# Two layers behind block-recurrent attention: units in the order of chunks, first products between the attention's steps, sums from parts, another planner

## The chip, the cores and the metric

One core of a Trainium2 chip. Five engines work side by side, each through its own queue in order: TensorE (PE; its weight loads are listed as PEld), VectorE (DVE), ScalarE (ACT), GpSimd (POOL) and SyncE (SP), which issues most loads. The metric is the time of one execution on the device in microseconds. The kernel before takes 581.78 us, the median of 3 runs (581.52 to 581.89).

## The reference

Blockwise linear attention with decay (2 batches, 8 heads, 768 positions, head size 64, blocks of 64), then two feed-forward layers (1536 tokens, 512 to 2048 to 512), all float32.

```python
for b in range(nb):                                   # 12 blocks of 64
    intra = einsum('bhic,bhjc->bhij', qb, kb) * Dmask
    intra = einsum('bhij,bhjd->bhid', intra, vb)
    inter = einsum('bhid,bhde->bhie', qb * lam_pow, kv_state)
    out[:, :, sl] = intra + inter
    kv_state = lam_block * kv_state + einsum('bhsd,bhse->bhde', kb * rev_pow, vb)
x = out.transpose(0, 2, 1, 3).reshape(1536, 512)
h = x @ w1i; x = where(h > 0, h, exp(min(h, 0)) - 1) @ w1o
h = x @ w2i; x = (max(h, 0) + alpha * min(h, 0)) @ w2o
```

## The kernel before

**The products.** A float32 operand is split into a high part, rounded to the fast format fp32r, and a low part, the rest (`split`, L385). A product is then three matmuls: high by high, high by low, low by high. The 1536 tokens are three chunks of 512, each of four tiles of 128 (`CHUNK`, L33: the tile numbers in the order in which they stand in the chunk; tiles 0 to 5 are batch 0, tiles 6 to 11 batch 1). The 2048 hidden columns are eight pairs j of two blocks of 128. An *up* step (`plain`, L794) is six matmuls of 128x128 by 128x512, half of one block of h; `finish` (L757) applies the layer's function and writes g, split into parts. A *down* step (`down`, L878) is six matmuls that add to acc. For j of 1 and more the up products of chunks 1 and 2 together are one two by two block product done with seven products instead of eight (`seven`, L836, table `PRODUCTS`); it needs the sums T1 to T4 of the blocks B11, B21 (chunk 1) and B12, B22 (chunk 2), which `combine` (L456) makes from the unsplit values in acc, working in place, split again into parts. T4 stands where B12 stood, so its split is made later (`late`).

**The attention.** Six units of 128 positions, each for both batches (`units`, m = 0 to 5; a unit is one tile of each batch). A unit has the steps scores (s, L557, masked on VectorE into sm), state (t, L604, the sum over the unit's keys and values, added to the decayed state st), outputs (o, L644) and earlier (i, L668, the part from the blocks before), each 64 matmuls of 64x64. `earlier` then evicts a bank of PSUM: a cast to the high part on ScalarE, the low part on VectorE, and for m below 4 a copy of the unsplit value to acc. Units 0 to 3 fill chunks 1 and 2, units 4 and 5 chunk 0. `attend` (L951) yields the steps in the order t0 o0 s1 i0 t1 o1 s2 i1 and so on; the last steps are merged one by one with the up steps of chunks 1 and 2 for pair 0. Then come `combine`, the down weights of pair 0, the rest of pair 0 and 1 for chunk 0, and `seven(0, 1)` among the down steps that are left.

**Order and queues.** `build` (L964) writes down all steps. `Plan` runs through them with a price for each: TensorE keeps the order as written, the other engines take what is needed first, in the order that the plan's clock gives. Loads of the first part are chained on SP's queue (`behind`): q, k and v of units 0 and 1, w1i of pair 0, units 2 to 5, w1o of pair 0. Tiles share memory by tags: a unit's tiles lie where g, x0, wa1, wd0, qT1 and qT2 come later, and the temporary ut where the powers of lam and the state st[3] are.

Of the kernel before, what the change touches and what calls it, by code (L numbers as in the profile page):

```python
# [32 lines left out]
CHUNK = [[4, 10, 5, 11], [0, 1, 2, 3], [6, 7, 8, 9]]  # L33
# [10 lines left out]
class Op:  # L44
    def __init__(self, costs, run, late, shared, dma):
        self.costs, self.run, self.late, self.shared, self.dma = costs, run, late, shared, dma
        self.least = min(costs.values())
        self.after, self.before = set(), []
        self.heir, self.waits = None, 0
        self.left = 0  # L50
        self.need = 0.0
        self.begun = False


class Plan:

    LAT = 0.12
    SPARE = 8.0  # L60
    EASE = 0.3
    HOLD = 8.0
# [6 lines left out]
    def add(self, costs, run, reads=(), writes=(), late=0.0, shared=False, dma=False):  # L69
        op = Op(costs, run, late, shared, dma)  # L70
# [12 lines left out]
    def behind(self, a, b):  # L83

        a.heir, b.waits = b, 1

    def needs(self):

        pe = [op for op in self.ops if "PE" in op.costs]
        behind = dict(zip(pe, pe[1:]))  # L90
        left = {}
        for op in self.ops:
            for a in op.after:
                a.before.append(op)
        for op in self.ops:
            left[op] = len(op.before) + (op in behind) + (op.heir is not None)
        todo = [op for op in self.ops if not left[op]]
        ahead = dict(zip(pe[1:], pe))
        first = {op.heir: op for op in self.ops if op.heir}
        n = 0  # L100
        while todo:
            op = todo.pop()
            n += 1
            ends = [s.need - (0.0 if "PE" in op.costs and "PE" in s.costs else self.LAT)
                    for s in op.before]
            if op in behind:
                ends.append(behind[op].need)
            op.need = min(ends, default=0.0) - op.least - op.late
            if op.heir:
                op.need = min(op.need, op.heir.need - op.least)  # L110
            for a in [*op.after, *([ahead[op]] if op in ahead else []),
                      *([first[op]] if op.waits else [])]:
                left[a] -= 1
                if not left[a]:
                    todo.append(a)
        assert n == len(self.ops)
        return pe

    def run(self):
        pe = self.needs()  # L120
        for op in self.ops:
            op.left = len(op.after) + op.waits
# [3 lines left out]
        events, n = [], 0  # L126
        at, done, now, dma, shift = 0, 0, 0.0, 0.0, -pe[0].need

        def offer(op):
            nonlocal n  # L130
            for e in op.costs:
                if e != "PE":
                    heapq.heappush(ready[e], (op.need, n, op))
# [7 lines left out]
        def begin(e, op):  # L141
            nonlocal dma
            op.begun = True
            op.run(e)
            if op.heir:
                op.heir.left -= 1
                if not op.heir.left:
                    offer(op.heir)
            cost = op.costs[e]
            free[e] = now + cost  # L150
# [3 lines left out]
            if op.dma:  # L154
                dma = max(dma, now + 1.6) + op.late
                wake(dma + self.LAT, op)
            else:
                wake(now + cost + (0.0 if e == "PE" else self.LAT), op)

        for op in self.ops:  # L160
            if not op.left:
                offer(op)
        while done < len(self.ops):
            for e in self.ENGINES:
                if free[e] > now + 1e-9:
                    continue
                if e == "PE":
                    if at < len(pe) and not pe[at].left:
                        shift = now - pe[at].need
# [4 lines left out]
                while ready[e]:  # L174
                    item = heapq.heappop(ready[e])
                    op = item[2]
                    if op.begun:
# [4 lines left out]
                    if e == "POOL" and any(  # L182
                            x.shared and not x.begun and x is not op and x.need < op.need
                            and x.need + shift < now + op.costs[e] + self.HOLD for _, _, x in ready["DVE"]):
# [3 lines left out]
                    slack = op.need + shift - now  # L188
# [922 lines left out]
```

## Time and profile before

| | |
|---|---|
| median of 3 runs | 581.78 us |
| the profiled execution | 581.23 us |
| its span, first to last instruction | 579.3 us |
| TensorE busy | 550.4 us, 95% |
| VectorE, ScalarE, GpSimd busy | 383.0, 293.1, 339.2 us |
| granted TensorE clock, mean | 0.982 |

The profile is one execution. Busy time is shown by engine; idle time stands beside what ended it, "issue" where the profile shows no wait. The span leaves out about 2 us around the first and last instruction.

### The profile page before, as it was taken

To read this page: it belongs to the slowest core of one execution; us is meant where nothing else is said; L and a number is where in the kernel's file an instruction comes from. 1 tells how busy PE (TensorE), PEld (TensorE's weight loads), DVE (VectorE), ACT (ScalarE), POOL (GpSimd) and SP (SyncE) were. 2 spreads that over 40 slices of the span, in tenths; PEclk is the share of its full clock that TensorE was granted. 3 is DMA by queue.
4 is the path that set the end of the run, shared out by engine and by line. 5 is a ranking of instruction groups with operands and counts; after the bars stand their busy time and mean duration, and the time that the engine had idled before them with its cause. 6 is when DMAs were issued, how large, how long until landed. Compare 5 with 4: busy or idle time off the path is not lost.

```text
span 579.3 us, 9092 instructions
## 1 busy us (share of the span) xinstructions
PE 550.4 (95%) x3712; PEld 457.1 (79%) x3712; DVE 383.0 (66%) x494; ACT 293.1 (51%) x474; POOL 339.2 (59%) x231
## 2 busy tenths in 40 slices
PE   7557999899999999999999999999999999999997
PEld 6457787788888888888878878788888888888886
DVE  3346679955866675757884688467776776765464
ACT  2326668585746464646562554664453443534320
POOL 4457152658767566564475886767859293946020
PEclk9778999999999999999999999999999999999999
DMA  8992032103122212221240100222332222000013
GB/s 320 393 291 77 20 129 74 46 30 143 41 106 74 72 74 72 74 72 74 72 147 1 35 39 1 73 74 73 98 120 74 72 74 72 1 0 1 36 38 145
DMA packets 20012, 49.62 MB, mean 86 GB/s; under 512 B 1282, under 2 KB 1538, under 8 KB 19970
## 3 DMA queue, kind: packets, MB, share of 16 engines
q1 hardware_dynamic: 19696, 48.51, 24.3%
q8 instruction: 29, 0.48, 0.3%
q10 hardware_dynamic: 274, 0.52, 0.3%
q14 instruction: 13, 0.11, 0.1%
HBM read 45.88 MB, written 3.15 MB: 85 GB/s over the span
## 4 chain that ended last, share of the span: by engine, by line
PE 85%; DVE 9%; issue 4%; DMA 1%; ACT 1%; SPq 0%; ACTq 0%
PE ps L895 41%; PE ps L845 20%; PE ps L815 18%; PE ps L668 2%; PE ps L604 1%; PE ps L557 1%; PE ps L644 1%; DMA blk<-in_vk 1%; DVE g L382 1%; DVE wt L413 1%; DVE qbl L382 1%; DVE wt L416 1%; DVE wdl L382 1%; DVE ps L859 1%; DVE acc L906 1%
## 5 line engine op out<-in xcount | busy, mean ns | idle before, releaser
L906 DVE TENSOR_TENSOR acc<-ps,acc 128x512 f32<-128x512 f32 (+1 forms) x169 | 116.1, 687 | 93.5 <-PE ps L895 92.6
L382 POOL TENSOR_TENSOR g<-rt,g 128x512 fp32r<-128x512 f32 x81 | 121.2, 1503 | 90.1 <-ACT g L374 88.0
L895 PE MATMUL ps<-wdh,g 128*128 128x512 f32 (+1 forms) x388 | 118.7, 387 | 1.4 <-DVE g L382 1.4
L895 PE MATMUL ps<-g,wdh 128*128 128x512 f32 x384 | 118.3, 389 | 0.0
L762 ACT ACTIVATE rt<-ps 128x512 f32<-128x512 f32 x96 | 57.3, 599 | 107.8 <-DVE ps L859 62.6
L895 PEld LDWEIGHTS ps<-wdh,g 128*128 128x128 f32 x388 | 72.7, 188 | 16.7 <-DVE g L382 1.9
L895 PEld LDWEIGHTS ps<-g,wdh 128*128 128x128 f32 x384 | 72.1, 188 | 15.0
L895 PE MATMUL ps<-wdl,g 128*128 128x512 f32 (+1 forms) x194 | 75.1, 387 | 0.0
L895 PE MATMUL ps<-g,wdl 128*128 128x512 f32 x192 | 74.8, 390 | 0.2 <-DVE wdl L382 0.2
L374 ACT CAST g<-rt 128x512 fp32r<-128x512 f32 x96 | 59.3, 618 | 28.7 <-DVE rt L775 14.4
L382 POOL TENSOR_TENSOR wsl<-wt,wsh 128x1024 fp32r<-128x1024 f32 x13 | 32.3, 2484 | 48.1 <-ACT wsh L374 30.5
L779 DVE SCALAR_TENSOR_TENSOR rt<-rt,beta,ps 128x512 f32<-128x512 f32 x48 | 35.7, 744 | 30.2 <-ACT rt L762 30.1
L382 POOL TENSOR_TENSOR wt<-wt 128x256 f32<-128x256 f32 x54 | 41.1, 778 | 10.4 <-DVE wt L416 4.8
L416 DVE SCALAR_TENSOR_TENSOR wt<-raw,wt 128x1024 uint32<-128x1024 uint32 x32 | 46.3, 1450 | 0.0
L413 DVE SCALAR_TENSOR_TENSOR wt<-raw,wt 128x1024 uint32<-128x1024 uint32 x32 | 45.6, 1429 | 0.2
L374 ACT COPY ut<-ps 128x512 f32<-128x512 f32 x42 | 24.6, 587 | 36.3 <-PE ps L845 36.1
L382 POOL TENSOR_TENSOR wdl<-wt,wdh 128x1024 fp32r<-128x1024 f32 x13 | 37.2, 2861 | 8.9 <-ACT wdh L374 8.7
L895 PEld LDWEIGHTS ps<-g,wdl 128*128 128x128 f32 x192 | 36.0, 188 | 7.9 <-DVE wdl L382 0.6
L895 PEld LDWEIGHTS ps<-wdl,g 128*128 128x128 f32 x194 | 36.4, 188 | 7.4
L859 DVE TENSOR_TENSOR ps<-ps,ut 128x512 f32<-128x512 f32 x42 | 29.2, 697 | 14.5 <-PE ps L845 14.3
L815 PE MATMUL ps<-x0l,wah 128*128 128x512 f32 x128 | 38.8, 389 | 0.0
L775 DVE SCALAR_TENSOR_TENSOR rt<-rt,ps 128x512 f32<-128x512 f32 x48 | 32.5, 681 | 8.7 <-ACT rt L773 8.0
(116 smaller groups left out, 948.6 us busy)
## 6 DMA issues: line engine op xcount, KB each, us to landing
raw<-in_w1i SPq DMA_DIRECT2D x8, 1024.0 KB, 5.5
raw<-in_w1o SPq DMA_DIRECT2D x8, 1024.0 KB, 4.9
raw<-in_w2i SPq DMA_DIRECT2D x8, 1024.0 KB, 5.5
raw<-in_w2o SPq DMA_DIRECT2D x8, 1024.0 KB, 4.9
blk<-in_kqT SPq DMA_DIRECT2D x11, 512.0 KB, 10.8
blk<-in_vk SPq DMA_DIRECT2D x10, 512.0 KB, 10.9
out<-acc SPq DMA_DIRECT2D x11, 256.0 KB, 2.0
blk<-in_kqT ACTq DMA_DIRECT2D x1, 512.0 KB, 5.3
```

Source lines behind the costliest of these rows:

```text
L374: nc.scalar.copy(dst(), src())
L382: lambda e: on(e).tensor_tensor(out=dst(), in0=a(), in1=b(), op=alu),
L413: op({"DVE": vec(1024)}, lambda e: nc.vector.scalar_tensor_tensor(out=tu, in0=lower, scalar=29, in1=tu, op0=ALU.logical_shift_right, op1=A ...
L416: op({"DVE": vec(1024)}, lambda e: nc.vector.scalar_tensor_tensor(out=tu, in0=upper, scalar=0x80000000, in1=tu, op0=ALU.bitwise_and, op1=A ...
L762: op({"ACT": act(512, True)}, lambda e: nc.scalar.activation(rt(i), h(), AF.Relu, scale=-1.0), [b_h], [b_r])
L775: op({"DVE": vec(512)}, lambda e: nc.vector.scalar_tensor_tensor(out=rt(i), in0=rt(i), scalar=-1.0, in1=h(), op0=ALU.add, op1=ALU.max), [b ...
L779: op({"DVE": vec(512) + 0.06}, lambda e: nc.vector.scalar_tensor_tensor(out=rt(i), in0=rt(i), scalar=beta[:, f:f + 1], in1=h(), op0=ALU.mu ...
L815: nc.tensor.matmul(out=banks[k], lhsT=wa(s, w)[:, cc, q * 128:(q + 1) * 128], rhs=(both[t][x] if t else x0(x))[:, cc, :], start=i == 0, st ...
L845: nc.tensor.matmul(out=banks[k], lhsT=left(s, a, w)[:, cc, :], rhs=quad(b, x)[:, cc, :], start=bool(opens and i == 0), stop=bool(closes an ...
L859: op({"DVE": vec(512)}, lambda e: nc.vector.tensor_tensor(out=banks[to], in0=banks[k], in1=ut(u), op=ALU.add), [b_ps[k], b_ut[u]], [b_ps[to]])
L895: nc.tensor.matmul(out=p_, lhsT=lhs, rhs=rhs, start=i == 0, stop=i == 5)
L906: op({"DVE": vec(w)}, lambda _, a=a, p_=p_: nc.vector.tensor_tensor(out=a(), in0=p_, in1=a(), op=ALU.add), [b_ps[k], *b_a], b_a)
```

## The change

The units go to the chunks in the order in which they are made: units 0 and 1 are chunk 1, units 2 and 3 chunk 2, units 4 and 5 chunk 0 as before. A written list, STEPS, sets the attention's steps with up steps (p) and down steps (d) of pair 0 for chunks 1 and 2 among them. w1o of pair 0 is loaded and converted ahead of unit 3. `earlier` no longer copies to acc; `combine_parts` adds high and low parts back together in the tiles of ut and makes T1 to T4 from those. Outputs always use banks 4 and 5. Units 2, 3 and 5 lie in other tiles. The planner gives TensorE an order of its own (FREE), counts instructions to be fetched (steps), goes forward and back through the plan six times and keeps the best by its own clock; SPARE and HOLD are smaller.

```diff
-CHUNK = [[4, 10, 5, 11], [0, 1, 2, 3], [6, 7, 8, 9]]
+CHUNK = [[4, 10, 5, 11], [0, 6, 1, 7], [2, 8, 3, 9]]
...
-    SPARE = 8.0
+    SPARE = 5.0
     EASE = 0.3
-    HOLD = 8.0
+    HOLD = 2.0
+    ROUNDS = 6
+    FETCH = 80.0
+    AHEAD = 512.0
+    FREE = True
     ENGINES = ("PE", "SP", "ACT", "DVE", "POOL")
...
+    def simulate(self, first, back=False, log=None):
+        pe = self.pe[::-1] if back else self.pe
+        before = (lambda op: op.after) if back else (lambda op: op.before)
...
+            if op.steps:
+                stock = min(self.AHEAD, stock + self.FETCH * (now - seen))
+                cost = max(cost, (op.steps - stock) / self.FETCH)
+                stock, seen = stock + self.FETCH * cost - op.steps, now + cost
...
+                if e == "PE" and self.FREE:
+                    while ready[e]:
+                        op = heapq.heappop(ready[e])[2]
+                        if op not in begun:
+                            shift = now - first[op]
+                            begin(e, op)
+                            break
+                    continue
                 if e == "PE":
...
+    def run(self):
+        self.pe = [op for op in self.ops if "PE" in op.costs]
+        for op in self.ops:
+            for a in op.after:
+                a.before.append(op)
+        first, best = self.needs(), None
+        for _ in range(self.ROUNDS):
+            log = []
+            begun, end = self.simulate(first, log=log)
+            if best is None or end < best[0]:
+                best = end, log
+            begun, end = self.simulate({op: -t for op, t in begun.items()}, True)
+            first = {op: -t - op.least - op.late for op, t in begun.items()}
+        for e, op in best[1]:
+            op.run(e)
...
-    in2 = [x[:, 2 * i:2 * i + 2] for x in
-           [sb("blk", [4, 512], F32, f"x0{p}") for p in range(2)] for i in range(2)]
-    in3 = [sb("blk", [2, 512], F32, t) for t in ("wa10", "wa11", "wd0h", "wd0l")]
-    in5 = [sb("blk", [2, 512], F32, t) for t in ("qT10", "qT11", "qT20", "qT21")]
-    b_in = {m: [Buf() for _ in range(4)] for m in (2, 3, 5)}
+    in_x = [x[:, 2 * i:2 * i + 2] for x in
+            [sb("blk", [4, 512], F32, f"x0{p}") for p in range(2)] for i in range(2)]
+    in_t = [sb("blk", [2, 512], F32, t) for t in ("qT10", "qT11", "qT20", "qT21")]
...
+    def combine_parts(o):
+        cols = slice(o * 256, (o + 1) * 256)
+        def tmp(i):
+            return ut(i).rearrange("p (c n) -> p c n", c=2)
+        def part(m, p):
+            return quad(m, p)[:, :, cols]
+        def whole(i, m):
+            sub(lambda: tmp(i), lambda: part(m, 0).bitcast(F32), lambda: part(m, 1).bitcast(F32),
+                [b_quad[m, 0, o], b_quad[m, 1, o]], [b_ut[i]], 512, alu=ALU.add)
+        def less(i, a, b):
+            sub(lambda: tmp(i), lambda: tmp(a), lambda: tmp(b), [b_ut[a], b_ut[b]], [b_ut[i]], 512)
+        def parts(m, i):
+            copy(lambda: part(m, 0), lambda: tmp(i), [b_ut[i]], [b_quad[m, 0, o]], 512, False)
+            sub(lambda: part(m, 1), lambda: tmp(i), lambda: part(m, 0).bitcast(F32),
+                [b_ut[i], b_quad[m, 0, o]], [b_quad[m, 1, o]], 512)
+        whole(0, "B12")
+        whole(1, "B11")
+        less(1, 0, 1)
+        parts("T1", 1)
+        whole(2, "B22")
+        less(0, 2, 0)
+        less(2, 2, 1)
+        parts("T2", 2)
+        parts("T3", 0)
+        whole(1, "B21")
+        less(1, 1, 2)
+        parts("T4", 1)
...
         return [(tiles[b], tiles[2 + b], bufs[b], bufs[2 + b]) for b in range(B)]
-    HOMES = [homes(blk[0:4], b_g[0:4]), homes(blk[4:8], b_g[4:8]), homes(in2, b_in[2]),
-             homes(in3, b_in[3]), homes(blk[0:4], b_g[0:4]), homes(in5, b_in[5])]
+    HOMES = [homes(blk[0:4], b_g[0:4]), homes(blk[4:8], b_g[4:8]), homes(in_t, b_t12),
+             homes(in_x, b_x), homes(blk[0:4], b_g[0:4]), homes(in_t, b_t12)]
+    PART = [1, 1, 2, 2, 0, 0]
...
-        i += 2 * (i == 4 and m in (1, 3))
...
-            op({"ACT": 1.55, "POOL": pool(512)}, decay, [b_st[old], b_qp],
+            op({"ACT": 1.55, "DVE": vec(512), "POOL": pool(512)}, decay, [b_st[old], b_qp],
...
-            if m < 4:
-                def dst(p, m=m, s=s):
-                    return pair[p].rearrange(
-                        "p b a (o s i) -> p b a o s i", s=2, i=C)[:, :, :, m, s, :]
-                def rest(m=m, s=s):
-                    return pair_acc.rearrange(
-                        "p b a (o s i) -> p b a o s i", s=2, i=C)[:, :, :, m, s, :]
-                b_hi, b_lo = [[b_quad[f"B{c}{t}", p, m // 2] for c in (1, 2) for t in (1, 2)]
-                              for p in range(2)]
+            t = PART[m]
+            def cols(x, s=s, u=m % 2):
+                return x.rearrange("p a (u b s i) -> p u b a s i", b=B, s=2, i=C)[:, u, :, :, s, :]
+            def dst(p, t=t, cols=cols):
+                return cols(both[t][p] if t else x0(p))
+            if t:
+                b_hi, b_lo = [[b_quad[f"B{c}{t}", p, m % 2] for c in (1, 2)] for p in range(2)]
             else:
-                def dst(p, m=m, s=s):
-                    return x0(p).rearrange("p a (o s i) -> p o a s i", s=2, i=C)[
-                        :, 2 * (m - 4):2 * (m - 3), :, s, :]
-                b_hi, b_lo = [[b_x0[p, 2 * (m - 4) + b] for b in range(B)] for p in range(2)]
+                b_hi, b_lo = [[b_x0[p, 2 * (m % 2) + b] for b in range(B)] for p in range(2)]
             copy(lambda dst=dst: dst(0), src, [b_ps[k]], b_hi, 512, True, ("ACT",))
-            if m < 4:
-                copy(rest, src, [b_ps[k]], [b_xr[m], b_ps[k]], 512, True)
             op({"DVE": vec(512)}, lambda e, dst=dst, src=src: nc.vector.tensor_tensor(
                 out=dst(1), in0=src(), in1=dst(0).bitcast(F32), op=ALU.subtract),
                [b_ps[k], *b_hi], b_lo)
...
-            finish(l, f, lambda k=k: banks[k], b_ps[k], (l, j, q, t), True)
+                x = pe(6 * MM, run, b_x + b_wa[s], [b_ps[k]])
+                if g:
+                    finish(l, f, lambda k=k: banks[k], b_ps[k], (l, j, q, t), True)
+                yield x
...
-            k = 5 + turn("dn", 3)
+            k = 6 + turn("fill", 2) if not (l or j) and t else 5 + turn("dn", 3)
...
-    def attend():
...
+    STEPS = ("t0 o0 s1 i0 t1 o1 i1 s2 p p t2 o2 p p i2 s3 d d t3 o3 d d i3 s4 t4 o4 p p p p i4 s5 "
+             "t5 o5 d d i5 d d").split()
     def build():
-        begin()
         def old(*bufs):
             return [o for b in bufs for o in b.read + b.wrote]
@@ -971,47 +1035,59 @@
                 x.load_kq("ACT" if m == 0 and i else "SP")
             for x in units[m]:
                 x.load_vk()
+        begin()
         fetch(0)
         fetch(1)
-        t_up = convert(0, 0, 0)
+        up = convert(0, 0, 0)
         fetch(2)
+        dn = convert(0, 0, 1)
         fetch(3)
         scores(0)
         scale(0)
-        steps = attend()
-        for i in range(23):
-            next(steps)
-            if i == 4:
+        ups = chain(plain(0, 0, 1), plain(0, 0, 2))
+        dns = downs(0, 0, [(t, e) for t in (1, 2) for e in range(4)])
+        ks = {}
+        for what in STEPS:
+            m = int(what[1:] or 0)
+            if what == "p":
+                next(ups)
+            elif what == "d":
+                next(dns)
+            elif what[0] == "t":
+                state(m)
+            elif what[0] == "o":
+                ks[m] = outputs(m)
+            elif what[0] == "i":
+                if m == 4:
+                    for b in b_x0.values():
+                        b.read += old(*b_x)
+                earlier(m, ks[m])
+            elif what[0] == "s":
+                scores(m)
+                scale(m)
+            if what == "i0":
                 fetch(4)
+            if what == "i1":
+                weights(0, 0, up)
+                weights_down(0, 0, dn)
+            if what == "o2":
                 fetch(5)
-        weights(0, 0, t_up)
-        for p in range(2):
-            for o in range(4):
-                b_x0[p, o].read += old(*b_in[2])
-        merge(chain(plain(0, 0, 1), plain(0, 0, 2)), steps)
+        for x in (ups, dns):
+            for _ in x:
+                pass
...
-        raw = [(acc[t], {(e, q): b_acc[t, e, q] for e in range(4) for q in range(2)})
-               for t in (1, 2)]
-        for q in range(2):
-            combine(0, 2, *raw, q)
...
-        weights_down(0, 0)
...
+                for o in range(2):
+                    combine_parts(o)
...
-                      chain(downs(0, 1, T0) if (l, j) == (0, 1) else (), downs(l, j - 1, T12),
+                      chain(downs(0, 1, T0) if (l, j) == (0, 1) else (),
+                            downs(l, j - 1, T12) if (l, j) != (0, 1) else (),
```

## Rows read from the trace of the kernel before

**Rows 1.** The page, first part: busy time, share of span, instructions.
```profile
PE 550.4 (95%) x3712; PEld 457.1 (79%) x3712; DVE 383.0 (66%) x494; ACT 293.1 (51%) x474; POOL 339.2 (59%) x231
```
**Rows 2.** Busy time by stretch: window, length, busy by engine, granted clock, DMA share, GB/s.
```profile
0.00:31.90 31.90, 20.48 (x558) 18.90 (x560) 12.85 (x33) 10.12 (x24) 15.88 (x22) 0.82 0.96 360
31.90:58.25 26.35, 16.20 (x689) 15.47 (x686) 13.14 (x19) 12.53 (x36) 16.29 (x12) 0.83 0.51 157
58.25:77.20 18.95, 18.70 (x291) 14.34 (x291) 13.15 (x17) 12.08 (x24) 7.27 (x5) 1.00 0.19 58
77.20:112.97 35.77, 34.05 (x150) 27.56 (x149) 32.34 (x42) 22.99 (x38) 14.21 (x10) 1.00 0.18 59
112.97:576.20 463.23, 460.98 (x2034) 380.79 (x2034) 311.08 (x386) 235.35 (x355) 285.58 (x186) 1.00 0.19 65
576.20:579.30 3.10, 0.00 (x0) 0.00 (x0) 0.42 (x1) 0.00 (x0) 0.00 (x0) 1.00 0.48 169
```
**Rows 3.** Waits of TensorE: its line, what ended them, total, times, longest.
```profile
PE ps L557 <- issue: 12.5, 5, 5.7
```
**Rows 4.** Timeline of TensorE, 21 to 59 us: start, length, instruction, [idle before <-releaser].
```profile
21.72 0.80 PE L604 MATMUL ps<-blk,kd 64*64 64x64 f32 x18 [3.21 <-issue]
...
28.19 0.80 PE L557 MATMUL ps<-blk 64*64 64x64 f32 x18 [2.77 <-issue]
...
34.47 0.50 PE L604 MATMUL ps<-blk,kd 64*64 64x64 f32 x18 [0.89 <-issue]
...
42.31 0.80 PE L557 MATMUL ps<-blk 64*64 64x64 f32 x18 [5.75 <-issue]
...
50.62 0.51 PE L557 MATMUL ps<-blk 64*64 64x64 f32 x19 [1.00 <-issue]
...
54.30 1.10 PE L604 MATMUL ps<-blk,kd 64*64 64x64 f32 x59 [1.23 <-DVE dmst L630]
...
58.25 0.57 PE L557 MATMUL ps<-blk 64*64 64x64 f32 x23 [1.28 <-issue]
```
**Rows 5.** The page, third part: the DMA queue of instructions, packets, MB, share.
```profile
q8 instruction: 29, 0.48, 0.3%
```
**Rows 6.** Busy time by stretches of 2 us, columns as in rows 2.
```profile
38.00:40.00 2.00, 0.00 (x0) 0.00 (x0) 0.00 (x0) 0.00 (x0) 0.00 (x0) 1.00 1.08 289
...
42.00:44.00 2.00, 1.69 (x43) 1.69 (x45) 0.86 (x3) 0.00 (x0) 0.00 (x0) 0.50 0.13 47
44.00:46.00 2.00, 2.00 (x42) 2.00 (x40) 1.22 (x3) 1.23 (x3) 0.34 (x1) 0.50 0.00 0
```
**Rows 7.** Timeline of TensorE, L668 twice; then a row of the chain (start, length).
```profile
42.91 3.41 PE L668 MATMUL ps<-qs,dmst 64*64 64x64 f32 x60
...
60.87 1.15 PE L668 MATMUL ps<-qs,dmst 64*64 64x64 f32 x32
...
120.05 1.36 PE ps L895 x6
```
**Rows 8.** Timeline of TensorE: outputs of unit 5, and the first product with T4.
```profile
68.86 1.16 PE L644 MATMUL ps<-sm,blk 64*64 64x64 f32 x64
...
112.97 0.70 PE L845 MATMUL ps<-qbh,wah 128*128 128x512 f32 x2 [1.56 <-DVE ps L859]
```
**Rows 9.** Timeline of SP's queue: the issue of w1o of pair 0.
```profile
32.90 0.50 SPq L362 DMA_DIRECT2D raw<-in_w1o  x1
```
**Rows 10.** Timelines of ScalarE, GpSimd and VectorE: an eviction, sums, conversion steps.
```profile
13.76 0.58 ACT L374 COPY acc<-ps 128x512 f32<-128x512 f32 x1
...
55.97 2.50 POOL L382 TENSOR_TENSOR acc<-acc 128x512 f32<-128x512 f32 x2
...
63.40 1.22 DVE L413 SCALAR_TENSOR_TENSOR wt<-raw,wt 128x1024 uint32<-128x1024 uint32 x1
...
73.97 2.68 DVE L413 SCALAR_TENSOR_TENSOR wt<-raw,wt 128x1024 uint32<-128x1024 uint32 x1
...
97.60 1.89 DVE L382 TENSOR_TENSOR acc<-acc 128x512 f32<-128x512 f32 x3
```

More of the change, by code (lines that the diff above doesn't have):

```diff
@@ L67, in __init__, with add @@
         self.ops = []
-    def add(self, costs, run, reads=(), writes=(), late=0.0, shared=False, dma=False):
-        op = Op(costs, run, late, shared, dma)
+    def add(self, costs, run, reads=(), writes=(), late=0.0, shared=False, dma=False,
+            steps=0):
+        op = Op(len(self.ops), costs, run, late, shared, dma, steps)
         for b in reads:
@@ L115, in needs @@
                     todo.append(a)
[L116 to L120, printed above, removed]
+        assert len(need) == len(self.ops)
+        return need
+    def simulate(self, first, back=False, log=None):
+        pe = self.pe[::-1] if back else self.pe
+        before = (lambda op: op.after) if back else (lambda op: op.before)
+        left = {op: len(op.before if back else op.after) for op in self.ops}
         for op in self.ops:
-            op.left = len(op.after) + op.waits
+            if (op.heir if back else op.lead):
+                left[op] += 1
         ready = {e: [] for e in self.ENGINES}
@@ L153, in begin @@
             wake(free[e])
-            if op.dma:
+            if back:
+                next_, gap = op.lead, cost
+            else:
+                next_, gap = op.heir, 0.0
+            if next_:
+                left[next_] -= 1
+                if not left[next_]:
+                    offer(next_)
+            if op.dma and not back:
                 dma = max(dma, now + 1.6) + op.late
@@ L157, in begin @@
             else:
-                wake(now + cost + (0.0 if e == "PE" else self.LAT), op)
+                wake(now + cost + op.late * back + (0.0 if e == "PE" else self.LAT), op)
         for op in self.ops:
-            if not op.left:
+            if not left[op]:
                 offer(op)
@@ L182, in run @@
                     if e == "POOL" and any(
-                            x.shared and not x.begun and x is not op and x.need < op.need
-                            and x.need + shift < now + op.costs[e] + self.HOLD for _, _, x in ready["DVE"]):
+                            x.shared and x not in begun and x is not op and first[x] < first[op]
+                            and first[x] + shift < now + op.costs[e] + self.HOLD
+                            for _, _, x in ready["DVE"]):
                         held.append(item)
@@ L203, in run @@
                 done += 1
-                for s in op.before:
-                    s.left -= 1
-                    if not s.left:
+                for s in before(op):
+                    left[s] -= 1
+                    if not left[s]:
                         offer(s)
+        return begun, now
+    def run(self):
[13 more added lines that the diff above has]
+            op.run(e)
 def act(n, psum=False):
@@ L560, in run @@
                             start=True, stop=True)
[L561 removed]
+            pe(ATT / 2, run, [x.b_kq], [b_ps[k] for k in ks], 64)
         for hs in range(2):
@@ L876, in seven, with close @@
                 finish(l, 2 * j + 1, lambda k=k: banks[k], b_ps[k], (l, j, 1, 1), True)
+    def close(l, e, t, a, b_a, cols, parts):
+        if l == 0:
+            hi, lo = [(both[t][p] if t else x0(p))[:, e, :] for p in range(2)]
+            m = f"B{1 + e // 2}{t}"
+            b_hi, b_lo = [[b_quad[m, p, o] for o in range(2)] if t else [b_y0[p][e]]
+                          for p in range(2)]
+            copy(lambda hi=hi: hi, a, b_a, b_hi, 512, False)
+            sub(lambda lo=lo: lo, a, lambda hi=hi: hi.bitcast(F32), b_a + b_hi, b_lo, 512)
+        if l == 1:
+            r0 = CHUNK[t][e] * TB
+            plan.add({"SP": 0.45}, lambda _, a=a, cols=cols, r0=r0: nc.sync.dma_start(
+                out=out[r0:r0 + TB, cols], in_=a()), b_a, [Buf()], late=0.7 / parts,
+                     dma=True)
     def down(l, j, t, e, parts=1):
```

129 lines of the change are left out of this document (45 added, 84 removed).

## The prediction, made before the result was known

> **What bounds the kernel now.** I read the page's engine table first: TensorE is busy 550.4 us of a span of 579.3 us [rows 1], so whatever is to be won lies in the 28.9 us in which it idles, and in matmuls that run at the low clock. The table by stretch says where [rows 2]. Its first line, up to the end of unit 1's part from earlier blocks at 31.90 us, idles 11.4 us; the second, up to 58.25 us, 10.15 us (26.35 less 16.20); the third 0.25, the fourth 1.72, the long fifth 463.23 - 460.98 = 2.25 us; behind the last matmul come 3.1 us of output. From 113 us on nearly nothing is left to win. The case is decided before 113 us.
>
> Next, what ends the idle time there. In the waits of TensorE the largest group is "issue": 12.5 us in 5 waits before L557 [rows 3]. "Issue" means that no semaphore was waited for. The timeline shows a pattern [rows 4]: counted with the shorter rows between them, 128, 127 and 128 matmuls lie between 21.72, 28.19, 34.47 and 42.31 us, that is 256 instructions, a weight load and a matmul each. The page's table of queues has one for instructions with 29 packets and 0.48 MB, about 16 KB each [rows 5], and 29 x 256 is the 3712 x 2 instructions of TensorE. So the instruction stream comes in blocks of 256, and TensorE waits for the next one. While the loads of q, k and v fill the DMA engines, a block takes 6.5, 6.3 and 7.8 us; after them, from 50.62 to 58.25 us, two blocks take 7.63 us, at most 3.8 us each [rows 4].
>
> A stall also costs the clock. Over 38 to 40 us TensorE does nothing at a DMA share of 1.08, and over 42 to 44 us its granted clock is 0.50, 1.2 GHz [rows 6]. Sixty matmuls of L668 take 3.41 us there, 32 of them 1.15 us later [rows 7]: 57 against 36 ns each.
>
> The Trainium skill ("Runtime: NRT & Kernel Launch", section on instruction fetch mechanics) gives the same block of 256 instructions, but says that crossing a block's border is mostly hidden. The trace disagrees for bursts of 64x64 matmuls and agrees for the dense 128x512 ones. By that rule the term for fetch below would be nil, and the sum 3 us lower.
>
> **The change, part by part.**
>
> *Order of units.* Before, chunks 1 and 2 each hold four tiles of one batch, and both are complete after unit 3 only. Now chunk 1 is complete after unit 1, chunk 2 after unit 3. No instruction is added. Unit 1's last part ends at 31.9 us before, behind scores of unit 2; now it stands ahead of them, and a little is gained that I leave out.
>
> *Sixteen steps moved into the attention.* Eight up steps and eight down steps of six matmuls, 1.36 us each [rows 7], 21.8 us in all. Before, the up steps began at 58 us and the down steps of chunks 1 and 2 came behind 94 us. They are no new work; they are worth what they cover. Take STEPS as it is written, with 1.1 us for 64 matmuls of scores, state or output and 2.16 us for a unit's earlier blocks [rows 7, 8]. Block borders then fall in t2, i2, t3, the second d d, s4, o4, s5 and the last d d, and the blocks hold 5.1, 5.4, 4.3, 3.7, 2.2, 8.3 and 3.5 us of matmuls. Against 3.8 us a block, stalls of 0.1, 1.6 and 0.3 us remain: 2.0 us. The first two blocks may still meet loads, at 6.4 us a block: another 1.3 and 1.0 us. The worst is 6.4 us for three blocks, 2.0 + 4.4. I take 3 us. Before, the same stretch had 10.15 us of idle, of which 5.75 and 0.89 us fall on blocks under load [rows 4].
>
> *The clock.* With no stall over about 1.6 us the second low stretch, 42.3 to 46.8 us, should go. TensorE is busy in nearly all of it [rows 6], so half of 4.4 us, 2.2 us, comes back. The first low stretch, from the stall that ends at 21.72 us, lies ahead of any filler and stays.
>
> *Loads.* w1o, 1 MB, moves ahead of unit 3 in SP's chain of loads. Before it was last, issued at 32.90 us [rows 9]. That delays units 3 to 5 by 1 MB at 360 GB/s [rows 2], 2.9 us. Unit 3 then lands around 28 us by bytes over that rate, and its scores ran at 35.8 us before, so this is covered; without the cover it costs up to 2.9 us. Unit 5's load now waits on SP for unit 2's tiles, free after o2 at about 36 us; 1.75 MB land by about 43 us and are wanted after 55. Behind it in SP's queue stand only weights of the second pair. The gap in loads helps the instruction blocks.
>
> *Copies and sums.* Eight evictions to acc of 0.58 us on ScalarE [rows 10] go (4.6 us). The sums are made from the high and low parts: 24 sums or differences of 128x512 where there were 16. On VectorE three of those took 1.89 us [rows 10], so the eight cost 5.0 us. They also start later. Before, the first ran on GpSimd at 55.97 us [rows 10]; now they write ut, whose tile holds st[3] and the powers of lam until unit 5 is finished, about 73 us. T1 is due about 12 up and down steps of chunk 0, B11, B21 and four downs later, 18 x 1.36 = 24.5 us on, T4 about 32 us on. All 24 take 15.1 us of VectorE; finishes, splits, the conversion of the third weights and adds ask for about 15 us more by my count of the groups there before (32.34 us busy in 35.77 us [rows 2]). So 30 us of work meet 32 us. Before, TensorE lost 1.56 us at the same place, waiting for VectorE behind T4 [rows 8]. I take 2 us (0 to 6).
>
> *Banks.* Outputs use banks 4 and 5 alone, so o(m+1) waits for the eviction of i(m), about 0.6 us on ScalarE and 0.7 on VectorE for each half; s, t or d steps lie between. One wait on VectorE inside the attention cost 1.23 us before, at 54.30 us [rows 4]. I take 1 us in all (0 to 2.5).
>
> *The other planner.* It orders TensorE freely and lets GpSimd begin sooner. The trace of before can't show that. It can win at most the 2.25 us of idle behind 113 us; the nearest row for a loss is 1.72 us in the crowded fourth stretch [rows 2], and three more changes of stage resemble it, so 5 us at worst. I take no change.
>
> **Sum**, from 31.9 us to the last matmul. Idle before: 10.15 + 0.25 + 1.72 + 2.25 = 14.4 us. After: 3 + 1 + 2 + 2.25 = 8.25 us. Gain 6.1 us, and 2.2 us of clock: 8.3 us. The profiled execution took 581.23 us, so 572.9 us; the median of the runs shown stands 0.55 us above it, so 573.4 us.
>
> **The rivals.**
>
> (a) *TensorE is kept full.* The planner spreads the steps over the blocks, and vector work is never late: idle falls to the 2.0 us of short blocks and 2.25 us, or less behind 113 us. Gain 10.1 + 2.2 = 12.3 us: 569.5 us, down to 566 with the last idle gone as well. For it: only 21.8 us of filler against 10 us of idle. Against: the fourth stretch. Chance 0.15.
>
> (b) *The stream stays the bound.* A free order takes attention steps as soon as they are ready and leaves the fill for the end; bursts stay bursts, weight loads of the second pair come early and keep blocks at 6.4 us, and the second low clock stays. Then 6.4 us of stalls and no clock gain: idle 11.65 us, gain 2.7 us, 579.1 us. For it: the pattern at 21.7 to 42.3 us. Against: the steps have no loads to meet after about 45 us. Chance 0.13.
>
> (c) *Slower: the sums from parts come too late.* Both halves go through the same three temporary tiles of ut, one behind the other: 2 x (12 x 0.63 + 4 casts of about 0.6) is 20 us at best, alone on VectorE. With every second sum on GpSimd, at 1.25 us [rows 10], it is 27.4 us. If each of the 24 links also waits behind one other instruction in VectorE's queue (finishes, conversions, adds) as long as a sum, it is 42.5 us; behind L413's 1.22 us [rows 10] at every second link, 49.6 us. T4 is due after 32 us, so it comes 10.5 to 17.6 us late, and from 10.3 us on (the 8.3 and the 2 counted already) the gain is gone: 582 to 589 us, 584 us taken. For it: the fourth stretch, where VectorE is busy 90% already, and L413, which takes 1.22 us alone and 2.68 us beside a subtraction on GpSimd [rows 10]. Against: the free order has eight up and down steps of the third weights to put in between. Chance 0.12. The Trainium skill ("GPSIMD Engine Reference", Specifications) names a contention of GpSimd with VectorE instructions that have two SBUF inputs, and every added sum is one; the two rows for L413 agree, and by that rule the sum would go toward this rival.
>
> (d) *Nothing moves.* The first block of fill is covered but paid back at T4, within 0.2% (about what a measurement of this kernel can tell from no change): 581 us. Chance 0.05.
>
> **How the numbers follow.** The forecast, 573.4 us, has 0.55 with its own bounds of 570 to 578. Faster by over 0.2% holds the forecast, (a) and (b): 0.83. Same 0.05, slower 0.12. The range leaves out about 0.06 below, the best end of (a), and 0.14 above, (c) and a part of (d): 566.5 to 580.5 us.
>
> **What would show it.** In the trace of after: 128x512 matmuls of up and down steps between L557 to L668's from about 32 us on; "issue" before TensorE halved or better, and the remaining part before 30 us; granted clock 1.00 from about 35 us on; the last matmul of attention at 72 to 75 us with 16 steps done; the first 128x512 sums into ut behind it; the first T4 product at 102 to 108 us, and idle there under 3 us. TensorE's busy time should fall by about 2 us. Wrong if idle of over 5 us stands ahead of T1 to T4, if the clock falls again past 36 us, or if the stretch behind 113 us loses more than 5 us.

## The result, and the profile after

The changed kernel takes 572.15 us, the median of 4 runs (571.17 to 573.72), against 581.83 us: a ratio of 0.9837, 95% interval 0.9813 to 0.9862, so 9.7 us or 1.6% faster. The forecast was 573.4 us with 566.5 to 580.5 us as the range. The time came out as forecast; most of the reason did not, as the runs below show, so the match is luck in the main.

The profiled execution took 572.72 us, with a span of 570.9 us. Its first line beside [rows 1]: TensorE is busy 1.9 us less, VectorE 13 us more.

```profile
PE 548.5 (96%) x3712; PEld 455.6 (80%) x3712; DVE 396.1 (69%) x515; ACT 287.1 (50%) x458; POOL 316.3 (55%) x220
```

Busy time by three stretches (columns as in [rows 2]), of the kernel before and of the changed one:

```profile
0.00:60.00 60.00, 38.38 (x1266) 35.48 (x1266) 27.13 (x53) 24.39 (x61) 32.38 (x33) 0.83 0.73 261
60.00:120.00 60.00, 58.07 (x443) 46.60 (x444) 47.47 (x59) 39.55 (x71) 26.98 (x18) 1.00 0.22 71
120.00:560.00 440.00, 437.76 (x1929) 361.53 (x1928) 299.41 (x370) 229.13 (x344) 279.87 (x180) 1.00 0.18 63
```

```profile
0.00:60.00 60.00, 41.40 (x1166) 37.26 (x1167) 39.01 (x63) 18.38 (x42) 27.75 (x29) 0.89 0.75 278
60.00:120.00 60.00, 59.78 (x572) 48.47 (x571) 51.43 (x66) 40.73 (x77) 13.47 (x10) 1.00 0.16 54
120.00:560.00 440.00, 439.55 (x1938) 363.32 (x1937) 301.02 (x381) 228.00 (x341) 275.05 (x182) 1.00 0.19 63
```

TensorE's idle time is the length less its busy time. It was 21.6, 1.9 and 2.2 us; it is 18.6, 0.2 and 0.45 us. So only 3.0 us of idle go in the first 60 us, where the forecast put all of its gain, and 3.5 us go behind, where it put none. Busy time, 1.9 us less, makes up the rest of the span's 8.4 us. This is one execution: a second trace of the same order of instructions (e7 below) idles 16.0 us in the first 60 us, and 0.2 and 0.5 us behind. From 31.9 us on, the stretch that the forecast summed, idle fell from 14.4 to 7.0 us (forecast: 8.25); ahead of it it grew from 11.4 to 12.3 us.

What TensorE waits for in the changed kernel (line, what ended the wait, total, times, longest):

```profile
PE ps L630 <- issue: 4.8, 2, 2.8
PE ps L717 <- DVE qbl L764: 4.0, 3, 2.6
PE ps L677 <- issue: 2.4, 1, 2.4
PE ps L741 <- issue: 1.7, 1, 1.7
PE ps L717 <- DVE sm L638: 1.6, 2, 0.8
PE ps L717 <- issue: 1.5, 1, 1.5
...
PE ps L978 <- DVE g L421: 0.2, 1, 0.2
```

"Issue" is 10.4 us here, 16.6 us before (L557 with 12.5 [rows 3], and L604):

```profile
PE ps L604 <- issue: 4.1, 2, 3.2
```

New are the waits of outputs (L717) for qbl, the low part of the unit before, which come from using banks 4 and 5 alone. Where they stand, in TensorE's timeline:

```profile
20.23 1.87 PE L717 MATMUL ps<-sm,blk 64*64 64x64 f32 x59 [2.58 <-DVE qbl L764]
...
27.62 0.40 PE L630 MATMUL ps<-blk 64*64 64x64 f32 x13 [2.76 <-issue]
...
33.85 0.71 PE L717 MATMUL ps<-sm,blk 64*64 64x64 f32 x17 [1.47 <-issue]
...
40.24 0.69 PE L677 MATMUL ps<-blk,kd 64*64 64x64 f32 x17 [2.43 <-issue]
...
41.72 2.07 PE L881 MATMUL ps<-qbh,wah 128*128 128x512 f32 x4
...
56.78 0.56 PE L741 MATMUL ps<-qs,dmst 64*64 64x64 f32 x12 [1.69 <-issue]
...
98.11 0.50 PE L978 MATMUL ps<-g,wdh 128*128 128x512 f32 x1 [0.22 <-DVE g L421]
```

The borders of blocks at 27.62, 33.85 and 40.24 us lie 6.2 and 6.4 us apart, as in [rows 4]: while loads run, instructions still set the pace at these places. The first up step starts at 41.72 us and not at 32, and the first four matmuls of the up steps take 2.07 us. The granted clock there, by stretches of 2 us:

```profile
34.00:36.00 2.00, 2.00 (x65) 2.00 (x66) 2.00 (x3) 0.22 (x2) 2.00 (x2) 0.50 1.03 394
...
38.00:40.00 2.00, 0.00 (x0) 0.00 (x0) 1.05 (x1) 0.00 (x0) 0.00 (x0) 1.00 1.02 368
40.00:42.00 2.00, 1.76 (x50) 1.64 (x51) 1.10 (x2) 0.31 (x2) 0.00 (x0) 0.60 0.69 211
42.00:44.00 2.00, 2.00 (x6) 1.57 (x6) 2.00 (x4) 0.97 (x4) 0.00 (x0) 0.55 0.56 189
```

TensorE does nothing from 38 to 40 us, and its granted clock is 0.60 and 0.55 of full speed over the next 4 us (half, 1.2 GHz, is the lower of its two levels), as before from 42 us on [rows 6]. The same stretches of the kernel before, at 34 and 46 us:

```profile
34.00:36.00 2.00, 1.53 (x104) 1.53 (x108) 0.99 (x2) 0.21 (x1) 2.00 (x3) 0.98 1.06 345
...
46.00:48.00 2.00, 2.00 (x86) 2.00 (x88) 2.00 (x2) 1.48 (x5) 2.00 (x2) 0.57 0.00 0
```

So the second low stretch is shorter, not gone, and one at 34 to 36 us is new.

### The profile page after: what moved, and what is told of

Its sections match the earlier page's. It is cut to its first block, busy times and chain, and to the rows that moved or that the text cites. A ratio compares the mean times of both kernels' runs of the same rounds, so it can differ in the third digit from the quotient of the medians.

```text
span 570.9 us, 9086 instructions
## 1 busy us (share of the span) xinstructions
PE 548.5 (96%) x3712; PEld 455.6 (80%) x3712; DVE 396.1 (69%) x515; ACT 287.1 (50%) x458; POOL 316.3 (55%) x220
## 4 chain that ended last, share of the span: by engine, by line
PE 89%; DVE 6%; issue 3%; ACT 1%; DMA 1%; SPq 0%; DVEq 0%; ACTq 0%
PE ps L978 44%; PE ps L913 22%; PE ps L881 16%; PE ps L741 2%; PE ps L717 2%; PE ps L630 1%; PE ps L677 1%; DMA blk<-in_kqT 1%; DVE ut L421 1%; DVE g L421 1%; DVE qT2l L421 1%; DVE sm L638 1%; DVE wt L455 0%; DVE acc L990 0%; DVE rt L845 0%
## 5 line engine op out<-in xcount | busy, mean ns | idle before, releaser
L421 POOL TENSOR_TENSOR wsl<-wt,wsh 128x1024 fp32r<-128x1024 f32 x12 | 29.9, 2493 | 40.9 <-ACT wsh L413 23.1
L421 POOL TENSOR_TENSOR wt<-wt 128x256 f32<-128x256 f32 x50 | 36.9, 746 | 23.4 <-DVE wt L455 10.6
L421 POOL TENSOR_TENSOR wdl<-wt,wdh 128x1024 fp32r<-128x1024 f32 x13 | 35.6, 2740 | 20.2 <-ACT wdh L413 20.0
L455 DVE SCALAR_TENSOR_TENSOR wt<-raw,wt 128x1024 uint32<-128x1024 uint32 x32 | 45.2, 1411 | 0.0
L452 DVE SCALAR_TENSOR_TENSOR wt<-raw,wt 128x1024 uint32<-128x1024 uint32 x32 | 44.7, 1397 | 0.2
L447 ACT ACTIVATE wt<-raw 128x1024 f32<-128x1024 f32 x32 | 36.4, 1139 | 5.1 <-POOL wt L421 4.5
```

Source lines behind the costliest of these rows:

```text
L421: lambda e: on(e).tensor_tensor(out=dst(), in0=a(), in1=b(), op=alu),
L447: op({"ACT": 1.14}, lambda e: nc.scalar.mul(t, upper.bitcast(F32), 2.0 ** -112), [b_r], [b_t])
L452: op({"DVE": vec(1024)}, lambda e: nc.vector.scalar_tensor_tensor(out=tu, in0=lower, scalar=29, in1=tu, op0=ALU.logical_shift_right, op1=A ...
L455: op({"DVE": vec(1024)}, lambda e: nc.vector.scalar_tensor_tensor(out=tu, in0=upper, scalar=0x80000000, in1=tu, op0=ALU.bitwise_and, op1=A ...
```

## The experiments

Two theories at the start. A, the forecast's: the gain comes from the up and down steps among the attention's steps. B: it comes from the planner. Times are medians; the kernel before took 581.5 to 581.9 us beside each group. The changed kernel is written "changed" here.

**The planner alone** (e1): the steps, tiles and banks of before, under the whole new planner.

```diff
-class Op / class Plan: as before
+class Op / class Plan: as in the change
-    ATT = 0.95
+    ATT = 0.88
```

> The steps, tiles and banks of the kernel before, ordered by the new planner alone (free order of TensorE, its prices for instruction fetch and for an attention step, six rounds, smaller SPARE and HOLD). Theory A, the forecast's: the gain comes from the up and down steps that stand in the attention, the planner adds nothing: 580 to 582.5 us. Rival B: the planner gives a good half of the gain, because the idle behind 77 us (1.72 and 2.25 us before, under 0.7 us in all in the changed kernel) goes with a free order: 576 to 579 us, and idle behind 77 us under 1.5 us in its trace.

574.5 us, ratio 0.9871 (0.9856 to 0.9887). **The steps alone** (e2): changed, with the old rules.

```diff
-    SPARE = 5.0;  HOLD = 2.0;  ROUNDS = 6;  FETCH = 80.0;  FREE = True;   ATT = 0.88
+    SPARE = 8.0;  HOLD = 8.0;  ROUNDS = 1;  FETCH = 1e9;   FREE = False;  ATT = 0.95
```

> The changed kernel's steps, tiles, banks and sums, with the rules of the planner before (TensorE in the written order, one pass, SPARE and HOLD 8, no price for fetch). Theory A: 572 to 575 us, all of the gain or nearly. Rival B: 576 to 580 us, the part that the attention gives and no more, and again over 2 us of idle behind 77 us.

580.81 us, ratio 0.9987 (0.9978 to 0.9997). Theory A falls: the steps alone, with the tiles, banks and sums that belong to them, bring 0.8 us, the planner alone 7.1 us. Both lie outside rival B's ranges too, which gave the planner less and the steps more. The stretches of e1, then of e2:

```profile
0.00:60.00 60.00, 39.94 (x1306) 37.41 (x1308) 28.33 (x55) 21.94 (x60) 26.74 (x30) 0.77 0.74 261
60.00:120.00 60.00, 60.00 (x430) 49.73 (x425) 48.70 (x64) 44.36 (x77) 23.31 (x17) 1.00 0.21 71
120.00:560.00 440.00, 439.58 (x1938) 363.33 (x1937) 298.00 (x374) 227.24 (x339) 275.36 (x180) 1.00 0.19 63
```

```profile
0.00:60.00 60.00, 43.38 (x1043) 36.98 (x1044) 37.65 (x58) 21.36 (x46) 29.32 (x31) 0.89 0.78 290
60.00:120.00 60.00, 54.81 (x683) 45.09 (x680) 41.34 (x55) 35.99 (x67) 25.13 (x19) 1.00 0.13 42
120.00:560.00 440.00, 436.60 (x1921) 359.94 (x1921) 306.81 (x383) 229.08 (x344) 275.98 (x178) 1.00 0.19 63
```

In e2 the steps do what the forecast said, for a while: idle in the first 60 us falls from 21.6 to 16.6 us. Then it comes back: 5.2 us between 60 and 120 us (1.9 before) and 3.4 behind (2.2 before). With TensorE held to the list, the fill has been spent when the rest of the attention must wait: 3.5 of the 5.2 us stand before steps of units 3 to 5. And the moved steps' own inputs come late. Two waits of e2:

```profile
PE ps L978 <- DVE g L421: 4.4, 3, 2.4
PE ps L881 <- DVE wah L415: 4.2, 1, 4.2
```

TensorE stands for 4.2 us before the first up step, for weights whose conversion VectorE ends at 33.8 us. In e1 no idle is left between 60 and 120 us and 0.4 us behind it.

**Fill behind the attention** (e4): the planner of the change, the sixteen steps written at the end of the list.

```diff
-    STEPS = ("... i1 s2 p p t2 o2 p p i2 s3 d d t3 o3 d d i3 s4 t4 o4 p p p p i4 s5 t5 o5 d d i5 d d")
+    STEPS = ("... i1 s2 t2 o2 i2 s3 t3 o3 i3 s4 t4 o4 i4 s5 t5 o5 i5 p p p p d d d d p p p p d d d d")
```

> The changed kernel with the sixteen up and down steps written behind unit 5's steps in the list, everything else kept. Theory A: the steps cover stalls and waits only where they stand among the attention's steps, so 4 to 7 us go again: 576 to 579 us, with issue before TensorE up by 3 us or more between 40 and 60 us. Rival B: the cover is worth little, because TensorE's own order had no up step ahead of 41.7 us in the changed kernel anyway: 572 to 574 us.

574.23 us, ratio 0.9877 (0.9859 to 0.9895): 2.1 us slower than changed and level with e1. Issue between 40 and 60 us rose from 1.7 to 3.5 us, not by 3. So under the new planner the written place of the steps is worth at most about 2 us. The whole plan is made anew in such a run, so a part of the 2 us may be that: in the profiled executions TensorE idles as long in e4 (572.1 less 549.9, 22.2 us) as in changed (570.9 less 548.5, 22.4 us). The edit also takes less away than it seems to. The free order pulls two of the up steps in among the attention's steps again, the first at 56.73 us, and in changed no more than four of the sixteen stand ahead of 58 us.

**Banks, planned anew** (e3), **and banks alone** (e7, e9). The forecast had 1 us for the single pair of banks.

```diff
     def two_banks(m, i):
+        i += 2 * (i == 4 and m == 1)
         return [i, i + 1]
```

> The changed kernel with outputs of unit 1 in banks 6 and 7 again (one line), the rest as it is. If the waits of outputs for the low part of the unit before (4.0 us in 3 waits, 2.6 us of it ahead of unit 1's outputs at 20.2 us) are a price of banks 4 and 5 alone: 2 to 3 us faster than the changed kernel, 569 to 570.5 us. If the instruction stream takes their place, since blocks come every 6.4 us while loads run: within 0.8 us of the changed kernel, with as much more issue before TensorE ahead of 30 us.

575.61 us, 3.5 us slower than changed although a constraint is gone. The waits for qbl fell to 2.0 us, those for the masks rose to 4.9 us: the new plan differs everywhere. One edit under such a planner shows the plan's scatter as much as the edit. So e7 was to keep every engine's order and change the banks behind it:

> The changed kernel with every engine's order exactly as it is there; only the outputs of unit 1 go to banks 6 and 7 after the order is fixed. So nothing but the wait of unit 1's outputs for the low part of unit 0 is taken away (2.6 us ahead of 20.2 us). If that wait is a price: 570 to 571.5 us, 1 to 2.5 us faster than the changed kernel. If the instruction stream, at 6.4 us a block while loads run, or unit 1's masks take its place: 571.5 to 573 us, and issue ahead of 30 us longer by as much.

In e7 the outputs of unit 1 had stayed in banks 4 and 5, so it is the changed kernel once more: 572.35 us, 570.42 to 574.22 in 5 runs, and 2.58 us of wait came out as 1.39 us in its trace. That trace has a span of 568.6 us, and its first 60 us show how far one order can differ from run to run:

```profile
0.00:60.00 60.00, 44.00 (x1176) 39.53 (x1176) 38.37 (x64) 20.64 (x48) 27.33 (x29) 0.83 0.76 278
```

e9 has the banks indeed:

```diff
+class Bank:                      # 4 or 5 while planning, 6 or 7 when the instructions are written
     def two_banks(m, i):
-        return [i, i + 1]
+        return [Bank(i), Bank(i + 1)] if i == 4 and m == 1 else [i, i + 1]
```

> The changed kernel, every engine's order exactly as it is there, with the outputs of unit 1 now indeed in banks 6 and 7 (in the run before of this purpose they had stayed in 4 and 5, so that it repeats the changed kernel, 572.35 us). Outputs of unit 1 then wait for their masks alone, not for the low part of unit 0 behind them on VectorE: 1.2 us earlier at about 20 us. If that is a price: 570.5 to 571.5 us. If the next block of instructions, due about 6.4 us behind the one before, ends last instead: 571.8 to 573 us, with issue ahead of 30 us longer by as much.

570.66 us (570.13 to 572.9), ratio 0.9813 (0.9794 to 0.9832), the best of all; 1.5 us under changed and 1.7 under its repetition, with ranges that overlap. Its timeline of TensorE:

```profile
19.12 1.55 PE L728 MATMUL ps<-sm,blk 64*64 64x64 f32 x46 [0.40 <-DVE sm L649]
...
21.76 0.69 PE L728 MATMUL ps<-sm,blk 64*64 64x64 f32 x14 [1.09 <-issue]
...
27.95 0.60 PE L641 MATMUL ps<-blk 64*64 64x64 f32 x13 [2.47 <-issue]
```

Unit 1's outputs start 1.1 us earlier, and then, after 46 of them, the next block of instructions ends last: the border after it comes at 27.95 us, against 27.62 in changed and 28.26 in e7. At this place the wait was hidden behind the instruction stream. Two profiled executions of one order differ by 2.3 us (spans of 570.9 us in changed, 568.6 us in e7), and e9's span, 568.4 us, is 0.2 us below e7's. In both e7 and e9 the clock is 1.00 from 40 us on and the first up step starts early (40.91 and 40.61 us). So the traces show 0.2 us for the bank; that the medians differ by more is not told apart from the spread of runs.

**Which rule of the planner?** Five runs: changed without the free order (e5), with one round (e10), with the old SPARE and HOLD (e11); before with the free order alone (e6), and with the free order and six rounds (e12). SPARE and HOLD, in us, share the work that both VectorE and GpSimd can do: VectorE leaves an operation that has more slack than SPARE, and GpSimd does not begin one while a more urgent one for VectorE is due within HOLD of its end. FETCH is the number of instructions that the planner counts on per us, ATT its price for an attention step. An operation's due time is when the planner wants it begun.

```diff
e5:  -    FREE = True            e10: -    ROUNDS = 6        e11: -    SPARE = 5.0;  HOLD = 2.0
     +    FREE = False                +    ROUNDS = 1             +    SPARE = 8.0;  HOLD = 8.0
e6 (on e1):  -  SPARE = 5.0;  HOLD = 2.0;  ROUNDS = 6;  FETCH = 80.0;  ATT = 0.88
             +  SPARE = 8.0;  HOLD = 8.0;  ROUNDS = 1;  FETCH = 1e9;   ATT = 0.95
e12 (on e1): the same, with ROUNDS = 6
```

> The changed kernel with TensorE held to the written order (FREE off), the other new rules kept: six rounds, small SPARE and HOLD, prices for fetch. If the free order is what the planner adds: near the steps with the old rules, 579 to 581 us. If it is the rounds and the other prices, which see that the weights of the first pair are wanted early: 572 to 575 us.

580.79 us, ratio 0.9986 (0.9971 to 1.0002): the gain is gone.

> The steps of the kernel before with the planner before but for one rule: TensorE takes what is ready and wanted first. One pass, SPARE and HOLD 8, no price for fetch, the old price for an attention step. If the free order is what the planner adds: 574 to 576.5 us, and idle behind 77 us under 1 us. If rounds, SPARE and HOLD carry it: 579 to 582 us.

580.51 us, ratio 0.9986 (0.9968 to 1.0005): a free order alone brings nothing that can be told from none.

> The changed kernel planned in one pass forward (ROUNDS 1) instead of the best of six; the free order, SPARE 5, HOLD 2 and the price for fetch stay. If the rounds, whose pass from the end back gives every instruction its due time with the other engines' load in it, are what the free order needs: 578 to 581 us, and TensorE again waits for VectorE's g, weights or T4 between 40 and 120 us. If SPARE and HOLD are what it needs: 571.5 to 574 us.

583.45 us, ratio 1.0024 (1.0011 to 1.0036): slower than before, and than expected. Between 40 and 120 us TensorE waits for the attention's low parts (qbl 2.6, x0l 1.3 us) and for instructions (2.0 us) and hardly for g (0.2 us).

> The changed kernel with SPARE and HOLD at 8 again, free order, six rounds and the price for fetch kept. If GpSimd's earlier start is what the free order needs: 576 to 581 us, GpSimd with less work and VectorE with more between 60 and 120 us. If the rounds are: 571.5 to 574.5 us.

573.65 us, ratio 0.9861 (0.9845 to 0.9878): these two are worth 1.5 us at most, within the plan's scatter.

> The steps of the kernel before, with its planner but for two rules together: TensorE's free order and the best of six rounds with a pass from the end back. SPARE and HOLD 8, no price for fetch, the old price for an attention step. If these two are the planner's gain: 573.5 to 576 us, near the whole new planner on these steps (574.5 us). If the price for fetch or SPARE and HOLD are needed as well: 577 to 581 us.

573.99 us, ratio 0.9871 (0.9853 to 0.9889). The free order and the rounds carry it; neither does by itself (the free order alone on both sets of steps, e6 and e10; the rounds alone on the changed steps, e5, and not tried on the old ones). The price for fetch, SPARE and HOLD aren't needed on the old steps. e12's stretches, then e10's:

```profile
0.00:60.00 60.00, 40.11 (x1326) 37.32 (x1326) 28.64 (x54) 22.67 (x58) 26.07 (x30) 0.77 0.74 261
60.00:120.00 60.00, 59.79 (x404) 48.72 (x401) 52.91 (x69) 44.15 (x75) 22.66 (x15) 1.00 0.20 71
120.00:560.00 440.00, 440.00 (x1942) 364.33 (x1942) 310.87 (x385) 226.83 (x339) 256.98 (x169) 1.00 0.19 63
```

```profile
0.00:60.00 60.00, 43.18 (x1054) 38.22 (x1054) 38.34 (x62) 22.75 (x53) 28.99 (x28) 0.86 0.75 278
60.00:120.00 60.00, 55.50 (x661) 45.34 (x660) 39.71 (x56) 33.97 (x60) 23.51 (x17) 0.97 0.15 46
120.00:560.00 440.00, 436.28 (x1914) 359.88 (x1913) 306.70 (x379) 229.58 (x345) 276.13 (x183) 1.00 0.19 64
```

e12 has 0.2 us of idle between 60 and 560 us; e10, with the same freedom and due times from one pass, has 8.2 us. How that looks in e10, on VectorE and then on TensorE:

```profile
32.39 1.90 DVE L455 SCALAR_TENSOR_TENSOR wt<-raw,wt 128x1024 uint32<-128x1024 uint32 x1
34.21 0.68 DVE L638 TENSOR_TENSOR sm<-ps,dmst 128x512 f32<-128x512 f32 x1
```

```profile
34.95 1.87 PE L717 MATMUL ps<-sm,blk 64*64 64x64 f32 x59 [2.69 <-DVE sm L638]
```

VectorE takes a conversion step of 1.9 us ahead of the mask that the attention waits for, and TensorE stands for 2.7 us. The first due times are counted from the end along the list, with no word of how busy the other engines are; the pass back through the plan puts their load in. That this is the way in which the rounds help is read from such rows; it was not measured by itself.

**The sums twice** (e8): every engine's order as in changed, each of the eight added sums done two times.

```diff
+            def add(e):
+                for _ in range(2):
+                    on(e).tensor_tensor(out=tmp(i), in0=part(m, 0).bitcast(F32), in1=part(m, 1).bitcast(F32), op=ALU.add)
```

> The changed kernel, every engine's order as it is there, with each of the eight sums from parts done twice: eight more sums of 0.6 to 1.3 us on VectorE and GpSimd between 80 and 100 us, where VectorE is busy 97%. If the sums are covered, as the forecast's 2 us say: within 1 us of the changed kernel. If VectorE is the bound there (the forecast's rival c): 4 to 6 us slower, with TensorE waiting for VectorE between 95 and 115 us.

576.84 us (575.97 to 580.7), 4.7 us slower than changed. Its largest wait on VectorE behind 60 us, VectorE just before it, and the clock behind it:

```profile
PE ps L982 <- DVE g L421: 2.9, 2, 2.4
```

```profile
95.35 1.77 DVE L421 TENSOR_TENSOR ut<-ut 128x512 f32<-128x512 f32 x1 [1.19 <-POOL ut L541]
97.04 1.74 DVE L421 TENSOR_TENSOR g<-rt,g 128x512 fp32r<-128x512 f32 x1
```

```profile
102.00:104.00 2.00, 2.00 (x6) 1.52 (x6) 1.91 (x4) 1.33 (x3) 0.00 (x0) 0.50 0.00 0
104.00:106.00 2.00, 2.00 (x7) 1.52 (x6) 1.97 (x4) 1.05 (x2) 0.00 (x0) 0.50 0.00 0
```

TensorE idles 3.45 us between 60 and 120 us, where changed has 0.22 us. It does not wait for T1 to T4; it waits for g, the result of an up step. But the chain of the sums is what makes g late: VectorE stands 1.2 us for a doubled sum on GpSimd, takes the difference that reads it, and only then g. In changed the same place shows the wait of 0.22 us at 98.11 us. The 3.2 us of idle are not the whole price: behind these waits the granted clock falls to half (0.94 on average over 60 to 120 us, 1.00 in changed) and is back at 1.00 from 108 us on. So the sums have little cover left: at the eight added sums 0.2 us of wait shows, eight more cost 4.7 us.

## Why the prediction was right, and where it wasn't

- *Time*: 572.15 us measured, 573.4 forecast; faster, as given 0.83.
- *Steps moved into the attention* (10.15 us of idle to become 3, and 1 for the banks): the step that failed. The forecast ran STEPS as the order of TensorE and asked what stalls remain; it priced the loads and took the other inputs of the moved steps (converted weights, g) for granted. Under that very order (e2) 5.0 us of idle went ahead of 60 us, in spite of an unpriced wait of 4.2 us for converted weights, and 4.4 us came back behind it. Under the new planner the steps are worth about 2 us at most (changed against e1 and e4).
- *The other planner* (no change, with 2.25 us of gain as the best): the term that was mis-sized most. It measured 7.1 us by itself. The bound was wrong in kind: it counted only idle behind 113 us as the planner's to win, though a free order can also win what stands ahead of it, and did: 21.6 + 1.9 + 2.2 us of idle became 20.1 + 0 + 0.4, and 3.5 us of that went ahead of 113 us (23.55 us of idle there before, 20.06 in e1).
- *The clock* (2.2 us back): not shown. The stall did not go; it ends at 40.24 us instead of 42.31, and the low stretch behind it is shorter, but another at 34 to 36 us has come. Busy time is 1.9 us less, the 2 us that the forecast gave as a sign; it is 1.5 us less in e7, and 0.2 us less in e9, whose mean clock over the first 60 us is the highest of the three (0.94). So the busy time of one execution does not measure this term.
- *Sums* (2 us, 0 to 6): 0.2 us of idle show at the place. The forecast's count of 30 us of work in 32 us was near: e8 shows that little is left over. Rival (c)'s price is real, at twice the sums, and its mechanism was half right: the chain through ut, with GpSimd in it, holds up VectorE, but TensorE feels it at g, behind the chain in VectorE's queue, and not at T4.
- *Banks* (1 us): 4.0 us of waits show, of which the largest was hidden behind the instruction stream; e9's trace is 0.2 us shorter than e7's.
- *Instruction blocks*: 6.2 to 6.4 us while loads run, as read before the change. Rival (b)'s stream did stay, up to 41 us, and so did a second low clock; and the free order left twelve of the sixteen steps behind 58 us, much as (b) had it. Its 579.1 us did not come: of the 4.7 us by which the idle time from 31.9 us on is under its 11.65, 3.6 us stand behind 60 us, where e1 shows that the planner alone wins as much.
- Of what was to show it: issue halved and the rest of it ahead of 30 us (10.4 of 16.6 us are left, three waits of it behind 30 us), up steps at 32 us (41.72), attention done at 72 to 75 us with sixteen steps (80.3, with twelve), the first T4 product at 102 to 108 us (117.76, with no wait) and a clock of 1.00 from 35 us on (0.55 to 0.60 at 40 to 44 us) came out wrong. The last is one of the forecast's own signs of being wrong.

So the sum was met, by luck, through two errors of about the same size with opposite signs: the moved steps with all that belongs to them 8.3 us forecast and about 2 measured, the planner 0 forecast and about 7 measured. (Taken in the other order, e2 first, the steps are worth 0.8 and the planner 8.7 us.) The rule on instruction fetch in the Trainium skill ("Runtime: NRT & Kernel Launch", instruction fetch mechanics) is that crossing a block's border is mostly hidden. The changed kernel's trace says of it what the trace before said: it disagrees ahead of 60 us, where 10.4 us of issue are left, and agrees behind, where there is none.

## What to carry to other kernels

Price an order change with its inputs: work moved forward fills a gap only if what it reads is ready there, and an in-order queue gives the gap back at the first input that is late. When a change contains a new scheduling rule, idle time anywhere is that rule's to win; run the old work under the new rule and the new work under the old one before crediting either. Under a planner that makes everything anew, single edits moved the time by 1.5 to 3.5 us here (e11, e4, e3), so freeze every engine's order when one cost is in question.

## What the runs showed of the hardware

A wait for VectorE can be hidden behind the instruction stream: with 0.40 us of wait at 20 us instead of 2.58 the next block's border came no earlier (27.95 and 27.62 us). A wait for VectorE can cost the clock as well: in e8 the granted clock was 0.50 over 102 to 106 us, behind three waits for g, 3.4 us in all. And one order of instructions gave 570.4 to 574.2 us in nine runs of changed and its repetition; in the two traces the granted clock is under 1.00 at other places (behind 10 us: 16 to 24, 32 to 38 and 40 to 44 us in one; 10 to 12, 14 to 26, 28 to 32 and 34 to 40 us in the other). What of the spread comes from that was not measured, and the column does not tell all of it. In e9 it reads 1.00 at 16 to 18 us, yet 30 matmuls take there what they take in changed at 0.50 (1.81 us at 35.19):

```profile
16.00:18.00 2.00, 2.00 (x62) 2.00 (x56) 1.04 (x2) 0.00 (x0) 1.92 (x2) 1.00 1.04 386
```

```profile
16.70 1.81 PE L752 MATMUL ps<-qs,dmst 64*64 64x64 f32 x30
...
46.27 1.09 PE L752 MATMUL ps<-qs,dmst 64*64 64x64 f32 x30
```
